# Attention, mixer and MLP block on one core: output-weight slices in other heads, and a rebuilt opening

## The chip, the cores and the metric

The kernel runs on one core of a Trainium2 chip. The metric is device time in microseconds (us), the median over several runs. The engines are named as the profile names them: PE is TensorE's matrix products, PEld its weight loads, DVE is VectorE, ACT is ScalarE, POOL is GpSimd and SP is SyncE, which here only issues DMAs. A name with a q (SPq) is the engine's own instruction queue. PSUM is the memory that TensorE writes its results to; everything else on the core lies in SBUF.

## The reference

The input x has 2048 rows of 640. A vector c gives six modulation rows of 640 through `silu(c) @ w_mod`. An attention with 32 heads over a given cache of 2048 keys follows, then a mixer and an MLP.

```python
mod = (_silu(c) @ w_mod).reshape(c.shape[0], 6, 1, -1)
sa, ca, ga, sb, cb, gb = (mod[:, 0].copy(), mod[:, 1].copy(), ...)
h = _layernorm(x, axis=-1) * (1 + ca) + sa
x = x + ga * _A_ref(h, A_k_cache, A_v_cache, A_wq, A_wo)
h = _layernorm(x, axis=-1) * (1 + cb) + sb
x = x + gb * _B_ref(h, B_w1, B_w2, B_w3, B_w4)
...
def _A_ref(x, k_cache, v_cache, wq, wo):      # H, Dh = 32, 128
    q = (lambda x, *d: x.transpose(*d))((x @ wq).reshape(B, Sq, H, Dh), 0, 2, 1, 3)
    scores = jnp.einsum('bhqd,bhkd->bhqk', q, k_cache) * Dh ** (-0.5)
    p = _softmax(scores, axis=-1)
    o = jnp.einsum('bhqk,bhkd->bhqd', p, v_cache)
    return (lambda x, *d: x.transpose(*d))(o, 0, 2, 1, 3).reshape(B, Sq, H * Dh) @ wo
```

`_B_ref` is a layernorm, a product with w1, GELU, a shift of column groups by one or two rows, a product with w2, and a second layernorm with the MLP (w3, GELU, w4).

## The kernel before

**Order of work.** A small class, `Prog`, takes operations for the five engines in program order, with the keys that each reads and writes, and turns every dependence between two engines into a semaphore wait. Within an engine the operations run in the order in which they were given. All loads and all transposes by DMA are issued from one queue, SP's; the writes of finished attention rows go out from POOL's queue.

**Attention.** The loop over `s` (L691) has 512 steps: 32 heads of 16 tiles of 128 query rows. In a step TensorE computes 128 x 2048 scores in two halves into PSUM (`qk`, L344); DVE scales each half into SBUF and takes its row minimum of the negated scores (L725); POOL joins the two minima (L735); ACT takes the exponential into the buffer `Pb`, eight steps deep (L738). The probabilities are transposed, mostly two steps at a time, by a DMA from SP's queue (`transpose`, L263); 8 to 10 steps later TensorE multiplies them with V (`pv`, L357), ACT copies the result out of PSUM (L679) and POOL normalises and stores it (L592, L599, L606). Beside the steps of one head stand the loads of the next ones (K at L748, the slice of wq at L750, V at L752) and the Q projection of the next head, in twenty pieces (`q_piece`, L277, emptied by ACT in `q_evac`, L284).

**The output weights.** `wo` (4096 x 640) is loaded in 16 slices of two heads each, 320 KB a slice (`load_wo`, L376). `WO_AT` (L688) says in which head, at step 11, which slice is issued: two in head 0, then one in every odd head from 1 to 27. Their space serves the opening first: the later part of w_mod, statistics and small vectors lie in it. Every operation that uses it so reads the keys `WRK`, and a slice's load waits for those.

**The opening** (L394 to L520) computes what the first scores need: layernorm statistics of x (`bn` and `aggr` on DVE, per tile two BATCH_NORM_STATS2 over 320 columns and one aggregate), the reciprocal root (`rs`: for the first four tiles Sqrt on ACT and a reciprocal on DVE, for the others two operations on POOL), the normalised rows (`xhat`), their transposes on TensorE (`tr`), and the modulated, transposed rows hT (`ev`, on ACT or DVE, from PSUM). `ev` needs the two modulation columns `mcol`: fifty small products on TensorE (`cols`, L423) from the first part of w_mod and silu(c), then two ACT operations (L509, L510). Then `q_head0` makes the first 512 columns of head 0's Q. Loads are issued in the order x(0), c, x(1), w_mod's first part, x(2), wq(0), K(0), x(3), wq(1), V(0), w_mod's rest; x(cc) is 512 rows, 640 KB. The vector c is loaded as 128 x 5 single elements.

**Head 0** carries the rest of that work as side work, placed by hand in the table `PLAN` (L327). Keys of `q1`, `own`, `mod` and `tr` are half steps `u` (two a step) in TensorE's queue: `q1` the Q pieces of head 1, `own` the remaining Q pieces of head 0, `mod` the modulation rows (`mod_rows`, L575), `tr` the transposes. `es` and `evv` place the evacuations on ACT and DVE; `bn` the statistics; `xv` and `xg` the normalisation of a tile on DVE or on POOL, by step. `within` (L522) runs a half step's TensorE part, `ahead` (L537) the ACT part before the step's exponential, `beside` (L547) the DVE and POOL part behind it.

**Tail.** From L764 on: the output projection, the mixer and the MLP, with TensorE busy almost throughout.

Of the kernel before, what the change touches and what calls it, by code (L numbers as in the profile page):

```python
# [151 lines left out]
def bass_adaLN_cond__mha_block_cached__mixer_s_mlp__prompt_kernel(  # L152
# [6 lines left out]
    KT = D // 128  # L159
# [14 lines left out]
    with ExitStack() as es:  # L174
# [11 lines left out]
        if True:  # L186
            with ExitStack() as es1:
# [44 lines left out]
                c_sb = wof[:, CO + 6 * KT:CO + 7 * KT]  # L232
                s_col = wof[:, CO + 7 * KT:CO + 8 * KT]
                assert CO + 8 * KT <= H * D and SK + 8 * D <= WO_ and WO_ + KT * 2 * D <= 10 * SK
# [85 lines left out]
                for cc in range(NQC):  # L320
# [84 lines left out]

                G.op("gpsimd", lambda g: g.memset(ident[:], 0.0), w=["id0"])
# [5 lines left out]
                eps_f, mh_f = pad[:, 0:4], pad[:, 4:8]  # L412
                G.op("gpsimd", lambda g: g.memset(eps_f, 0.0), w=["warm"])
                G.op("gpsimd", lambda g: g.memset(mh_f, -0.5), w=["mh"])
                G.op("scalar", lambda a: a.activation(s_col, c_sb, ACT.Silu), r=["c"], w=["scol"])
                G.op("scalar", lambda a: a.activation(c_f, c_sb, ACT.Silu), r=["c"], w=["cf"])
# [19 lines left out]
                def aggr(cc):  # L436
                    for t in range(4 * cc, 4 * cc + 4):
                        G.op("vector", lambda v, t=t: v.bn_aggr(mv[:, t, :], st[:, t, :]),
                             r=[("st", t, 0), ("st", t, 1)] + WRK, w=[("mv", t)])

                def rs(cc):
                    c4 = slice(4 * cc, 4 * cc + 4)
                    if cc == 0:
                        G.op("scalar", lambda a: a.activation(sd[:, c4], mv[:, c4, 1], ACT.Sqrt, bias=float(EPS)),
                             r=[("mv", t) for t in range(4 * cc, 4 * cc + 4)], w=[("sd", cc)])
                        G.op("vector", lambda v: v.reciprocal(rstd[:, c4], sd[:, c4]), r=[("sd", cc)], w=[("rstd", cc)])
                    else:
                        G.op("gpsimd", lambda g: g.tensor_scalar(out=sd[:, c4], in0=mv[:, c4, 1], scalar1=float(EPS), scalar2=1.0,
                                                                 op0=ALU.add, op1=ALU.mult),
# [51 lines left out]
                for k in range(KT - 1):  # L501
                    tr(0, (k,), Sps[:, k * 512:(k + 1) * 512].bitcast(BF16), ("Sb", k))
# [571 lines left out]
```

## Time and profile before

| | us |
|---|---|
| median of 3 runs | 1537.18 (1533.27 to 1546.02) |
| the profiled execution | 1542.95 |
| its span, first to last instruction | 1541.2 |
| first attention reduction on DVE (L725) | 20.55 from the span's start |
| first one of head 1 | 66.01 |
| start of the last of all | 1211.6 |

The profile is of one execution. The page lists the busy time of each engine; the other views are questions to the same trace: its instructions in order of time, busy time by stretch, who waited for whom (total us, times, longest), and the DMA issues with the time from issue to landing. An instruction is written as engine, line, operation, output<-input; in the view by time the first number is its start and the second its length in us, and instructions of one kind that follow each other are merged (x4). A wait for several semaphores is put down to the one that came last. The granted TensorE clock was 1.000 throughout.

The loads of the opening, from the DMA issues of short stretches: x(0) issued at 0.74, landed 4.2 later; c at 1.25, 5.3; x(1) at 1.80, 6.9; w_mod's first part at 2.36, 10.4; x(2) at 2.91, 11.5; wq(0) at 4.47, 10.5; K(0) at 6.12, 10.8; x(3) at 14.91, 4.9.

### The profile page before, as it was taken

How to read it: one execution, taken by the hardware profiler on the slowest of the kernel's cores; microseconds unless marked ns; L12 is line 12 of the kernel's file. 1: busy time of each engine (PE TensorE's matmuls, PEld its weight loads, DVE VectorE, ACT ScalarE, POOL GpSimd, SP SyncE). 2: the span in 40 equal slices, each digit the busy share in tenths (PEclk: the TensorE clock that was granted, in tenths of full speed). 3: DMA queues.
4: the chain of work that ended last, by engine and by line, in shares of the span. 5: the costliest groups of instructions: out<-in, count | busy, mean ns of one | idle time of the engine just before them, and what ended most of it. 6: DMA issues, size and time to landing. Idle time of an engine off the chain costs nothing.

```text
span 1541.2 us, 36159 instructions
## 1 busy us (share of the span) xinstructions
PE 1491.6 (97%) x14087; PEld 951.2 (62%) x14087; DVE 1372.1 (89%) x2425; ACT 1240.7 (81%) x1141; POOL 644.7 (42%) x1409
## 2 busy tenths in 40 slices
PE   5999999999999999999999999999999999999999
PEld 2566666666666666666666666666666665544444
DVE  8999999999999999999999999999999556676324
ACT  6999999999999999999999999999999500044230
POOL 4344444444444444444444444444444433332100
PEclk9999999999999999999999999999999999999999
DMA  9999999999999999999999999999999997635100
GB/s 280 226 244 227 250 257 249 247 251 249 253 244 255 242 251 248 253 248 258 243 242 256 251 252 253 260 253 254 263 243 225 226 219 169 131 85 105 34 17 35
DMA packets 1187333, 337.08 MB, mean 219 GB/s; under 512 B 1167984, under 2 KB 1181232, under 8 KB 1187248
## 3 DMA queue, kind: packets, MB, share of 16 engines
q1 hardware_dynamic: 1181104, 319.31, 99.6%
q0 software_dynamic: 6144, 16.79, 3.9%
q8 instruction: 35, 0.57, 0.2%
q14 instruction: 50, 0.41, 0.1%
HBM read 43.48 MB, written 19.40 MB: 41 GB/s over the span
## 4 chain that ended last, share of the span: by engine, by line
ACT 28%; DVE 25%; PE 24%; DMA 11%; issue 11%; POOL 0%; SPq 0%; ACTq 0%; DVEq 0%; POOLq 0%
DVE negS L725 24%; ACT ring L738 22%; DMA ring<-ring 9%; PE Sps L795 9%; PE Sps L996 4%; ACT ring L306 2%; ACT Of L679 2%; PE Oaug L980 2%; PE QPp L980 2%; PE PTp L364 2%; ACT kv L287 1%; PE Sps L962 1%; PE Sps L351 1%; DMA hTx<-o_scratch 1%; PE QPp L867 1%
## 5 line engine op out<-in xcount | busy, mean ns | idle before, releaser
L725 DVE TENSOR_SCALAR_CACHE_REDUCE negS<-Sps 128x1024 f32<-128x1024 f32 x1024 | 1174.7, 1219 | 10.8 <-PE Sps L351 10.0
L738 ACT ACTIVATE ring<-negS,small 128x2048 bf16<-128x2048 f32 x512 | 1039.2, 2050 | 23.5 <-DMA ring<-ring 11.4
L364 PEld LDWEIGHTS PTp<-kv,ring 128*128 128x128 bf16 x8192 | 555.9, 98 | 259.6 <-issue 14.0
L364 PE MATMUL PTp<-kv,ring 128*128 128x129 bf16 x8192 | 644.1, 220 | 15.0 <-DMA ring<-ring 13.8
L351 PE MATMUL Sps<-kv 128*128 128x512 bf16 x2048 | 616.8, 383 | 15.4 <-DVE negS L725 5.6
L735 POOL TENSOR_SCALAR small<-small 128x1 f32<-128x1 f32 x512 | 147.2, 287 | 570.5 <-DVE negS L725 570.3
L351 PEld LDWEIGHTS Sps<-kv 128*128 128x128 bf16 x2048 | 132.3, 97 | 149.9 <-DVE negS L725 125.0
L599 POOL TENSOR_SCALAR On<-Of,small 128x128 bf16<-128x128 f32 x512 | 192.0, 376 | 13.0
L592 POOL TENSOR_TENSOR small<-Of,small 128x4 f32<-128x4 f32 x128 | 133.2, 1041 | 22.5 <-ACT Of L679 22.5
L280 PE MATMUL Oaug<-hTx,kv 128*128 128x512 bf16 x320 | 120.5, 381 | 1.4 <-ACT hTx L481 1.4
L606 POOL DMA_DIRECT2D o_scratch<-On x128 | 103.2, 806 | 40.8 <-POOL On L599 37.2
L679 ACT COPY Of<-PTp 128x259 f32<-128x259 f32 x256 | 104.6, 409 | 18.9 <-PE PTp L364 18.9
L280 PE MATMUL QPp<-hTx,kv 128*128 128x512 bf16 x320 | 119.2, 378 | 0.6 <-DMA kv<-in_A_wq_dram 0.6
L875 ACT ACT_TABLE_LOAD x1 | 1.3, 1283 | 104.2 <-POOL hTx L923 104.2
L725 DVE DVE_READ_ACCUMULATOR negS<-Sps 128x1 f32 x1024 | 84.8, 83 | 0.0
L776 POOL TENSOR_SCALAR negS<-negS 128x1 f32<-128x1 f32 x48 | 24.1, 503 | 118.2 <-DVE negS L785 118.0
L795 PE MATMUL Sps<-wo,hTx 128*128 128x512 bf16 (+1 forms) x512 | 70.5, 299 | 0.2 <-DMA hTx<-o_scratch 0.2
L1013 DVE TENSOR_TENSOR ring<-Sps,ring 128x640 f32<-128x640 f32 x15 | 12.4, 824 | 65.5 <-PE Sps L996 65.5
L795 PE MATMUL Sps<-wo,negS 128*128 128x128 bf16 (+1 forms) x512 | 70.4, 299 | 0.0
L807 DVE TENSOR_TENSOR ring<-Sps,mod_bc 128x640 f32<-128x640 f32 x16 | 13.1, 821 | 51.3 <-PE Sps L795 51.3
L795 PEld LDWEIGHTS Sps<-wo,negS 128*128 128x128 bf16 x512 | 39.6, 98 | 30.4
L795 PEld LDWEIGHTS Sps<-wo,hTx 128*128 128x128 bf16 x512 | 39.4, 98 | 30.3 <-DMA hTx<-o_scratch 0.4
(99 smaller groups left out, 994.7 us busy)
## 6 DMA issues: line engine op xcount, KB each, us to landing
kv<-in_A_v_cache_dram SPq DMA_DIRECT2D x32, 512.0 KB, 4.9
o_scratch<-On POOLq DMA_DIRECT2D x128, 128.0 KB, 5.2
ring<-in_A_x_dram SPq DMA_DIRECT2D x8, 640.0 KB, 5.0
kv<-in_A_wq_dram SPq DMA_DIRECT2D x32, 160.0 KB, 3.2
wo<-in_A_wo_dram SPq DMA_DIRECT2D x16, 320.0 KB, 5.3
ring<-ring SPq DMA_TRANSPOSE x254, 6.5
wo<-in_w_mod_dram SPq DMA_DIRECT2D x1, 3200.0 KB, 15.0
out_dram<-wo SPq DMA_DIRECT2D x16, 160.0 KB, 1.8
```

What stands on the lines that cost most here:

```text
L280: G.op("tensor", lambda t: t.matmul(JB[jb], wq[:, hb, q, :], hT[:, q, cc * 512:(cc + 1) * 512], start=(q == 0), stop=(q == KT - 1)), r=[(" ...
L351: ins = t.matmul(Sps[:, col:col + 512], QT[:, hb, j * 128:(j + 1) * 128], KTs[:, hb, col:col + 512], start=True, stop=True)
L364: ins = t.matmul(ob[:, 0:129], PTs[:, b, kt, :], Vaug[:, hb, kt, 0:129], start=(kt == 0), stop=(kt == NKT - 1))
L592: G.op("gpsimd", lambda g: g.tensor_tensor(out=rl[:, 4 * b:4 * b + 4], in0=Of[:].rearrange("p a z d -> p (a z) d")[:, 4 * b:4 * b + 4, 128 ...
L599: G.op("gpsimd", lambda g: g.tensor_scalar(out=On[:, b, z, :], in0=Of[:, 2 * b + z // 2, z % 2, 0:128], scalar1=rl[:, 4 * b + z:4 * b + z ...
L606: G.dma("gpsimd", lambda e: e.dma_start(o_scr[jj // 2:jj // 2 + 2, :, hh].rearrange("a p z d -> p a (z d)"), On[:, b].rearrange("p (a z) d ...
L679: G.op("scalar", lambda a: a.copy(Of[:, p % 4].rearrange("p z d -> p (z d)")[:, 0:259], PO[:, (p % 2) * 512:(p % 2) * 512 + 259]), r=[("O" ...
L725: G.op("vector", lambda v, half=half, s=s, r8=r8: v.tensor_scalar(out=negS[:, s % 3, half * 1024:(half + 1) * 1024], in0=Sps[:, half * 102 ...
L735: G.op("gpsimd", lambda g, r8=r8: g.tensor_scalar(out=nm[:, r8:r8 + 1], in0=nm0[:, r8:r8 + 1], scalar1=nm1[:, r8:r8 + 1], scalar2=None, op ...
L738: G.op("scalar", lambda a, s=s, r8=r8: a.activation(Pb[:, s % RPB, :], negS[:, s % 3, :], ACT.Exp, bias=nm[:, r8:r8 + 1], scale=-1.0), r=[ ...
L795: ins = t.matmul(YB[b][:, c0:c0 + cw], OTj[pr % 2][:, 2 * hh + z, :], wo[:, hh, c0:c0 + cw], start=(hh == 0), stop=(hh == H - 1))
L980: ins = t.matmul(JB[jb][0:fsz[f_], :], w3[:, k, f_ * 128:f_ * 128 + fsz[f_]], nT[:, k, cc * 512:(cc + 1) * 512], start=(k == 0), stop=(k = ...
```

## The change

Four parts:

1. **Slices.** `WO_AT` issues the 16 slices in heads 5, 6, 8, 9, 11, 12 and so on to 26, 27, one a head.
2. **Loads.** x(0), x(1) and x(2) are issued first, then c, w_mod's first part, wq(0), x(3), K(0) and the rest as before. c is loaded as five rows of 128, turned into columns by one TensorE transpose (`c_cols`), and the two Silu read PSUM. 
3. **Statistics.** For tiles 3, 6, 7 and 11 ACT sums the row (Identity with an accumulator), POOL makes the negative mean, ACT sums the squares of x plus that (Square with an accumulator), and POOL makes mean and variance. The reciprocal root of the first four tiles moves to POOL's two operations, so ACT's Sqrt and DVE's reciprocal go. Twenty-four products of the identity with itself (`warm`) are put in TensorE's queue, ten ahead of c's transpose and fourteen behind it. The order of the opening is rewritten; the s columns that `mod_rows` needs (`spread_s`) move behind the third group's statistics on POOL, mcol's two copies behind ACT's last sum of squares; the first group's evacuations are three on DVE and two on ACT instead of two and three; tile 12's statistics come into the opening, and the second group's transposes and evacuations leave it.
4. **Table.** `PLAN` is new: the second group's transposes at half steps 0 and 1 with their five evacuations on ACT in step 0; DVE normalises tiles 8, 11, 14, 15 and 13, POOL 10, 9 and 12 (before: DVE 8, 11, 15; POOL 10, 9, 12, 13, 14); statistics of 13 to 15 in steps 2 and 3; Q pieces and modulation rows moved by a few half steps.

```diff
+                def junk():
+                    nj[0] += 1
+                    assert nj[0] <= NJ
+                    return wof[:, JU + (nj[0] - 1) * D:JU + nj[0] * D]
...
-                    q1={0: (3, 4, 6, 6, 7), 1: (14, 16, 16, 16, 17), 2: (15, 17, 17, 17, 17), 3: (25, 26, 29, 30, 30)},
-                    own={1: (2, 2, 3, 5, 5), 2: (10, 11, 12, 12, 12), 3: (22, 22, 22, 23, 23)},
-                    mod=[(9, 3, 2), (11, 2, 1), (14, 3, 0), (16, 3, 1), (18, 2, 1)],
-                    tr={0: (1, (4,), 1), 6: (2, (0, 1), 2), 7: (2, (2, 3), 1), 8: (2, (4,), 0), 18: (3, (0, 1), 0), 19: (3, (4,), 2), 21: (3, (2, 3), 1)},
-                    es={0: [(1, (4,))], 3: [(2, (2,)), (2, (0,)), (2, (1,))], 4: [(2, (3,))], 10: [(3, (4,))]},
+                    q1={0: (3, 4, 4, 5, 7), 1: (14, 14, 15, 16, 17), 2: (15, 15, 16, 16, 16), 3: (26, 28, 30, 30, 31)},
+                    own={1: (2, 3, 4, 5, 5), 2: (10, 11, 11, 12, 12), 3: (22, 22, 22, 22, 23)},
+                    mod=[(9, 3, 2), (12, 3, 1), (14, 3, 0), (16, 2, 1), (18, 2, 1)],
+                    tr=[(0, 1, (0, 1), 2), (0, 1, (4,), 2), (1, 1, (2, 3), 0), (6, 2, (0, 1), 2), (7, 2, (2, 3), 1), (8, 2, (4,), 0), (19, 3, (0, 1), 0), (19, 3, (4,), 2), (21, 3, (2, 3), 1)],
+                    es={0: [(1, (0, 1, 2, 3)), (1, (4,))], 3: [(2, (0,)), (2, (1,)), (2, (2,))], 4: [(2, (3,))], 10: [(3, (4,))]},
                     evv={4: [(2, (4,))], 9: [(3, (0,)), (3, (1,))], 10: [(3, (2, 3))]},
-                    bn={1: (12,), 2: (13, 14, 15)},
-                    xv={0: (8, 11), 8: (15,)},
-                    xg={0: (10,), 1: (9,), 3: (12,), 5: (13,), 7: (14,)},
+                    bn={2: (13, 14), 3: (15,)},
+                    xv={0: (8,), 1: (11,), 7: (14, 15), 8: (13,)},
+                    xg={0: (10,), 1: (9,), 4: (12,)},
...
-                    with nc.allow_non_contiguous_dma(reason="tiny c vector"):
-                        return e.dma_start(c_sb, c[0].rearrange("(kt p) -> p kt", p=128))
-                load_x(0)
+                    return e.dma_start(c_row, c[0].rearrange("(k p) -> k p", p=128))
+                for cc in range(3):
+                    load_x(cc)
                 G.dma("sync", load_c, "c", w=["c"])
-                load_x(1)
                 load_mod(0, wmod, 0, 2 * D)
-                load_x(2)
                 load_wq(0)
+                load_x(3)
                 load_k(0)
-                load_x(3)
...
+                def c_cols():
+                    G.op("tensor", lambda t: t.transpose(ctr, c_row, ident[0:KT, 0:KT]), r=["c", "ident"] + WRK, w=[("J", 0)])
+                    G.op("scalar", lambda a: a.activation(s_col, ctr, ACT.Silu), r=[("J", 0)] + WRK, w=["scol"])
+                    G.op("scalar", lambda a: a.activation(c_f, ctr, ACT.Silu), r=[("J", 0)] + WRK, w=["cf"])
+
+                def warm(n, key):
+                    def f(t):
+                        for _ in range(n):
+                            ins = t.matmul(JB[0][:, 0:128], ident[:], ident[:], start=True, stop=True)
+                        return ins
+                    G.op("tensor", f, r=["ident", key], w=[("J", 0)])
+
+                def sum_x(t):
+                    dst = junk()
+                    G.op("scalar", lambda a: a.activation(dst, xs(t), ACT.Identity, accum_out=sums[0][:, t:t + 1]),
+                         r=[("x", t // 4)] + WRK, w=[("sum", t)])
+
+                def sum_sq(t):
+                    dst = junk()
+                    G.op("scalar", lambda a: a.activation(dst, xs(t), ACT.Square, bias=sums[1][:, t:t + 1], accum_out=sums[2][:, t:t + 1]),
+                         r=[("x", t // 4), ("nmean", t)] + WRK, w=[("ssq", t)])
+
+                def nmean(t0, t1):
+                    G.op("gpsimd", lambda g: g.tensor_scalar(out=sums[1][:, t0:t1], in0=sums[0][:, t0:t1], scalar1=-1.0 / D, scalar2=1.0,
+                                                             op0=ALU.mult, op1=ALU.mult),
+                         r=[("sum", t) for t in range(t0, t1)] + WRK, w=[("nmean", t) for t in range(t0, t1)])
...
-                bn(0, 4)
-                aggr(0)
+                bn(0, 3)
+                aggr(0, 3)
+                sum_x(3)
+                nmean(3, 4)
+                sum_sq(3)
+                mean_var(3, 4)
                 rs(0)
+                warm(10, ('mv', 1))
+                sum_x(6)
+                sum_x(7)
+                sum_x(11)
+                c_cols()
+                warm(14, ('mv', 1))
+                nmean(6, 8)
+                nmean(11, 12)
+                sum_sq(6)
+                sum_sq(7)
+                mean_var(6, 8)
+                bn(4, 6)
+                aggr(4, 6)
+                rs(1)
                 xhat("vector", 0, 4)
+                tr0()
+                bn(8, 11)
                 G.op("scalar", lambda a: a.activation(eps_f, eps_f, ACT.Exp), r=["warm"], w=["warm"])
...
+                sum_sq(11)
+                mean_var(11, 12)
+                mcol_of()
+                aggr(8, 11)
+                rs(2)
                 spread_s()
...
+                xhat("vector", 4, 6)
+                ev("vector", 0, (0, 2, 4))
+                ev("scalar", 0, (1, 3))
                 q_head0(0)
...
+                xhat("vector", 6, 8)
+                bn(12, 13)
...
-                WO_AT = {0: (0, 1), **{h: (h // 2 + 2,) for h in range(1, 2 * NWP - 4, 2)}}
+                WO_AT = {5 + i // 2 * 3 + i % 2: (i,) for i in range(NWP)}
```

`mean_var` is two POOL operations that scale the two sums by 1/640 into the tile's mean and variance; `mcol_of` holds the column products and the two ACT operations as before; `tr0` the first group's transposes as before.

More of the change, by code (lines that the diff above doesn't have):

```diff
@@ L411, in bass_adaLN_cond__mha_block_cached__mixer_s_mlp__prompt_kernel @@
                 G.op("gpsimd", lambda g: g.memset(Vaug[:, :, :, 128:130], 1.0), w=["ones"])
[L412 to L416, printed above, removed]
+                ctr = JBb[0][:, 0:KT]
@@ L442, in rs @@
                     c4 = slice(4 * cc, 4 * cc + 4)
[L443 to L449, printed above, removed]
[L450 to L452 removed]
+                    G.op("gpsimd", lambda g: g.tensor_scalar(out=sd[:, c4], in0=mv[:, c4, 1], scalar1=float(EPS), scalar2=1.0,
+                                                             op0=ALU.add, op1=ALU.mult),
+                         r=[("mv", t) for t in range(4 * cc, 4 * cc + 4)], w=[("sd", cc)])
+                    G.op("gpsimd", lambda g: g.tensor_tensor(out=rstd[:, c4], in0=sd[:, c4], in1=mh_f, op=ALU.pow),
+                         r=[("sd", cc), "mh"], w=[("rstd", cc)])
                 def xhat(eng, t0, t1):
@@ L494, in q_head0, with mcol_of, tr0 @@
                         q_evac(0, cc)
-                bn(0, 4)
-                aggr(0)
-                rs(0)
+                def mcol_of():
+                    G.op("tensor", cols, r=["scol", ("wm", 0)] + WMK + WRK, w=[("J", 1)])
+                    G.op("scalar", lambda a: a.copy(mcol[:, 0:KT], JB[1][:, 0:KT]), r=[("J", 1)], w=["mcol0"])
+                    G.op("scalar", lambda a: a.add(mcol[:, KT:2 * KT], JB[1][:, KT:2 * KT], 1.0), r=[("J", 1), "mcol0"], w=["mcol"])
+                def tr0():
+                    for k in range(KT - 1):
+                        tr(0, (k,), Sps[:, k * 512:(k + 1) * 512].bitcast(BF16), ("Sb", k))
+                    tr(0, (KT - 1,), OB[0], ("O", 0))
@@ L554, in beside @@
                         if t == NQT - 1:
-                            aggr(3)
+                            aggr(12, 16)
                             rs(3)
```

54 lines of the change are left out of this document (25 added, 29 removed).

## The prediction

> **What bounds the kernel now.** I began with the page's busy shares. They are an average over an opening, 512 attention steps and a tail on TensorE, so I read stretches next.
>
> ```profile
> PE 1491.6 (97%) x14087; PEld 951.2 (62%) x14087; DVE 1372.1 (89%) x2425; ACT 1240.7 (81%) x1141; POOL 644.7 (42%) x1409
> ```
>
> ```profile
> 658.00:807.00 149.00, 144.54 (x1483) 97.02 (x1480) 146.83 (x257) 145.58 (x129) 70.03 (x160) 1.00 1.20 247
> ...
> 954.00:1101.00 147.00, 145.86 (x1498) 96.93 (x1496) 147.00 (x259) 147.00 (x129) 70.05 (x161) 1.00 1.20 255
> ```
>
> Columns: length, then busy time of PE, PEld, DVE, ACT, POOL. From 954 to 1101 DVE has no idle time: attention runs at DVE's pace, two reductions a step. The timeline shows that pace, and where it starts:
>
> ```profile
> 20.55 1.17 DVE L725 TENSOR_SCALAR_CACHE_REDUCE negS<-Sps 128x1024 f32<-128x1024 f32 x1
> ```
>
> ```profile
> 998.98 1.22 DVE L725 TENSOR_SCALAR_CACHE_REDUCE negS<-Sps 128x1024 f32<-128x1024 f32 x1
> ...
> 1001.27 1.22 DVE L725 TENSOR_SCALAR_CACHE_REDUCE negS<-Sps 128x1024 f32<-128x1024 f32 x1
> ```
>
> A step is 1001.27 - 998.98 = 2.29 us. The same view has head 1's first reduction at 66.01. Head 0 takes 66.01 - 20.55 = 45.46, of which 16 x 2.289 = 36.62 is its reductions and 8.84 side work and idle time. From 66.01 to the start of the last reduction (1211.6) there are 495.5 steps: 1134.2 at that pace, 1145.6 in fact, so 11.4 us of stalls. The waits name them:
>
> ```profile
> PE PTp L364 <- DMA ring<-ring: 13.8, 19, 1.2
> ```
>
> TensorE's second product waits for the transposes of the probabilities, and DVE then waits for the next scores (10.0 us in 20 waits). The tail from 1212.8 on is bound by TensorE and is not touched. So the change can act in three places: the 20.55 us before the first reduction, head 0's 8.84, and the 11.4 of stalls.
>
> **The opening.** DVE before the first reduction: 8 statistics 3.25 + 3.24 + 3.24 (three groups of four tiles), aggregates 3 x 0.41, reciprocal 0.18, xhat 1.52 + 1.51, two evacuations 0.99: 15.2 us after x lands at 4.94. After: statistics of nine tiles (0 to 2, 4, 5, 8 to 10, 12) at 0.81, 7.3; eight aggregates at 0.10, 0.8; eight xhat, 3.0; three evacuations, 1.5: 12.6. If DVE never waited, the first reduction would start at 17.6, a gain of 2.9.
>
> DVE now depends on ACT, whose rows before are
>
> ```profile
> 6.94 1.28 ACT L444 ACT_TABLE_LOAD   x1
> 8.57 0.20 ACT L444 ACTIVATE small<-small 128x4 f32<-128x4 f32 x1 [0.34 <-DVE small L438]
> 8.79 1.28 ACT L500 ACT_TABLE_LOAD   x1
> 10.09 0.20 ACT L500 ACTIVATE pad<-pad 128x4 f32<-128x4 f32 x1
> ```
>
> The next row starts at 14.33, so ACT was idle for 4 us there. After, in its order: sum and square of tile 3, sums of 6, 7, 11, two Silu behind a table load, squares of 6 and 7, the Exp load, square of 11, then mcol's two copies. A pass over 640 elements with an accumulator is in no row. From below: 512 elements cost 0.59 (the Q evacuation) and 2048 cost 2.00, so 640 cost 0.71. From above: the 512-element evacuation with two pointer operands at 0.77, plus 0.12 for the length, plus 0.08 as DVE pays to read its accumulator: 0.97. I take 0.80, nearer to the lower end, since the 2048-element row reads SBUF as these do. The chain: 4.96 + 5 x 0.80 + 0.3 (POOL's 0.20 for the negative mean, and two hand-offs) = 9.3; load and Silu 1.28 + 0.4 = 10.9; two squares 12.5; Exp 1.28 + 0.2 = 14.0; square of 11 14.8; mcol at 15.2, where it was at 14.70.
>
> TensorE's 50 column products (1.49) wait for the first part of w_mod. Its queue:
>
> ```profile
> ring<-in_w_mod_dram SPq DMA_DIRECT2D x1, 1600.0 KB, 10.4
> ...
> wo<-in_c_dram SPq DMA_DIRECT2D x1, 1.2 KB, 5.3
> ```
>
> ```profile
> 4.00:5.00 1.00, 0.00 (x0) 0.00 (x0) 0.04 (x1) 0.00 (x0) 0.00 (x0) 1.00 0.65 143
> 5.00:6.00 1.00, 0.00 (x0) 0.00 (x0) 1.00 (x3) 0.00 (x0) 0.00 (x0) 1.00 0.57 121
> ```
>
> The last column is GB/s. While c's 1.2 KB is loaded element by element the queue moves some 130, against 420 from 8 to 9: 1.4 us lost. As five rows that loss goes (at worst it stays); the third x load, now ahead of w_mod, adds 655 KB / 410 = 1.6. So w_mod lands at 12.76 + 0.2 = 12.9, at worst 14.4, and the columns end at 14.4 to 15.9. K of head 0, which landed at 16.9, has the fourth x load moved past it on SP (+1.6) and c's loss taken out: 17.0, at worst 18.5.
>
> From mcol at 15.2: evacuations 1.5 (DVE three, ACT two), last Q product and its evacuation 0.4 + 0.6, hand-offs 0.1, scores 0.6: 18.4. DVE, after its evacuations, does xhat of 6 and 7 and tile 12's statistics (0.76 + 0.81) and ends at 18.3. So the first reduction would start at 18.4; with 0.97 per pass 1.4 later, with w_mod at worst 0.7 later. I take 19.0, as hand-offs between five engines are likelier to add than to save: **-1.5 us**, bounds -2.8 (0.71 a pass) and 0 (both at their worst).
>
> Waits it adds: on ACT, Silu waits for c's transpose, which on TensorE stands behind ten warming products waiting for tile 1's aggregate (7.7); behind Silu stand the squares, Exp and mcol. On POOL the negative mean of 11 waits for x's third load, and behind it are the variances of 6 and 7 and the power (1.05, row of the 128x4 power) that releases xhat 4 and 5: 12.5 + 0.4 + 0.2 + 1.05 = 14.2, before DVE's evacuations can start at 15.2, so hidden by one us. The power for tiles 0 to 3 replaces a table load, Sqrt and reciprocal (1.7 together): even. The s columns move on POOL behind three such groups and end near 19; their first reader ran at 34.17. Warming products and memsets fill idle time: nothing, and at most 24 x 0.117 (the first 16 transposes took 1.87) = 2.8 if the tiles' transposes were ready at once.
>
> **Head 0.** DVE gets two more xhat (0.4 to 0.6 each) and one tile's statistics fewer (-0.81): 0 to +0.4. Five evacuations of the second x group (0.70 each) now stand on ACT ahead of the first Exp, which starts near 23.0 instead of 23.44: ACT gains less than DVE. It has 3.7 us idle from 24 to 60, so it can follow, but TensorE's shared PSUM banks are emptied by ACT, and 20 transposes (1.5) join its steps. The new table's idle time is in no row: -1.0 to +1.5. I take **+0.3**.
>
> **The slices.** Two leave head 0, one each heads 1 and 3; the rest stand in two heads of three from 5. On SP's queue, two cycles from V to V:
>
> ```profile
> 919.88 0.59 SPq L253 DMA_DIRECT2D kv<-in_A_v_cache_dram  x1
> 920.50 1.40 SPq L377 DMA_DIRECT2D wo<-in_A_wo_dram  x1
> ...
> 956.69 0.59 SPq L253 DMA_DIRECT2D kv<-in_A_v_cache_dram  x1
> ...
> 992.48 0.60 SPq L253 DMA_DIRECT2D kv<-in_A_v_cache_dram  x1
> ```
>
> 36.81 with a slice, 35.79 without: a slice costs the queue about 1.0, and the queue is full against a head of 36.62. By head 4 the queue has carried four slices fewer; from 5 to 27 it carries two in three heads instead of one in two. Stalls may fall by up to 4 x 1.0, or rise by (2/3 - 1/2) x 1.0 x 23 = 3.8. What is saved early is mostly paid late: **-0.5**.
>
> **Sum.** -1.5 + 0.3 - 0.5 = -1.7. The profiled execution took 1542.95 (span 1541.2), which gives 1541.2; it lies 5.8 above the median of three runs, 1537.18. I apply the difference to the median: **1535.5**.
>
> **Rivals.** (1) ACT's chain becomes the bound, and it is slower. Square stands after Silu and again after Exp; rows show that Identity and Copy run after Exp with no new load, none shows it for Square. Three more loads at 1.28 put mcol at 19.0, 3.2 later the first reduction at 22.2 and, with head 0 and the slices as above, the end 1.5 later than before: 1539. It decides from the second such load on (21.0 against 20.55). Against it: the simple functions have needed no load so far. Chance 0.17. (2) The denser slices keep the transposes late through heads 5 to 27: +3.8, with the opening's gain 1540. For it: heads around 480 to 810 stall with slices; against it: heads without slices stall too. 0.12. (3) The early slices were what began the lag, and nearly all stalls go. The fastest run before, 1533.27, is 9.7 below the profiled one and so has few; less 1.7 that is 1531.5. 0.13. (4) The opening is rebuilt but w_mod and K land at their worst and it gains nothing: 1537, 0.07. [...] Chance 0.03. [...]
>
> **Numbers.** Forecast 0.48, rivals 0.17, 0.12, 0.13, 0.07 and 0.03. About 1%, 15 us, is what a measurement of this kernel can tell from no change (three runs spread over 13). No case reaches it: within 0.95; 0.02 faster and 0.03 slower for what I have not named. The range takes (3) with the best opening, 1528, and (2) with the spread of the runs, 1545.
>
> **What would show it.** First reduction near 19.0 (after 20.5: the opening failed); mcol near 15.2; one table load for Silu and one for Exp, none for Square; nine tiles of statistics on DVE before it; head 0 within 45.5 to 46.5; no slice before head 5 on SP, and 7 to 12 us of stalls after head 0. I am wrong if one wait in head 0 passes 3 us, or if stalls leave 3 to 16.

## The result, and the profile after

The kernel after takes 1531.66 us (median of 22 runs, 1530.67 to 1542.33), the kernel before 1540.53 on the same chips (22 runs, 1531.96 to 1550.10). The ratio is 0.9956, with a 95% interval of 0.9938 to 0.9973: a gain that the measurement resolves, but one of less than 1%.

The single times say more than the medians. Of before's 22, seven lie within 1531.96 to 1533.68 and fifteen from 1537.18 up. Of after's 22, twenty lie within 1530.67 to 1532.59. The bulk of the gain is thus that long executions have become rare; between the best groups of the two kernels there is about 1 us.

The profiled execution after took 1531.64 (span 1529.8); before's span was 1541.2. Cut at the same places as in the prediction, the 11.4 us between the two spans come from:

| | before | after | difference |
|---|---|---|---|
| first reduction on DVE | 20.55 | 20.20 | -0.35 |
| head 0, first reduction to head 1's first | 45.46 | 45.78 | +0.32 |
| head 1's first reduction to the end of the last | 1146.8 | 1135.9 | -10.9 |
| the tail behind it | 328.4 | 327.9 | -0.5 |

496 steps at 2.289 us are 1135.3, so 0.6 us of stalls are left where before had 11.5. In before, the 30 heads from 1 to 30 exceed 16 steps of 2.289 (36.62 us) by 9.4 in all, the longest taking 38.18; in after each of them takes 36.62. The busy times of the page, and the two stretches of attention that the prediction read (length, then busy time of PE, PEld, DVE, ACT, POOL, then granted clock, DMA share, GB/s):

```profile
PE 1476.2 (96%) x13867; PEld 948.8 (62%) x14112; DVE 1368.0 (89%) x2415; ACT 1249.1 (82%) x1155; POOL 640.8 (42%) x1418
```

```profile
658.00:807.00 149.00, 145.65 (x1486) 98.13 (x1511) 149.00 (x261) 149.00 (x131) 71.59 (x164) 1.00 1.16 255
954.00:1101.00 147.00, 143.66 (x1468) 96.81 (x1492) 147.00 (x259) 147.00 (x130) 70.03 (x161) 1.00 1.16 255
```

In the first stretch DVE was idle for 2.17 us before, and is not idle now. The waits of after no longer have a line for TensorE's second product waiting on the transposes (13.8 us in 19 waits before), and DVE's wait for scores is down from 10.0 us in 20 waits to this (total, times, longest):

```profile
DVE negS L787 <- PE Sps L362: 2.8, 3, 1.3
```

L787 is the reduction that was L725, L362 the score products. One of the three stands late in head 0 (0.65 at 56.83), two in the opening, as its DVE rows show (start, length, and in brackets the idle time ahead of it and what ended that):

```profile
18.06 0.87 DVE L477 BATCH_NORM_STATS2 wo<-ring 128x6 f32<-128x320 bf16 x2
20.20 1.22 DVE L787 TENSOR_SCALAR_CACHE_REDUCE negS<-Sps 128x1024 f32<-128x1024 f32 x1 [1.28 <-PE Sps L362]
...
22.34 1.22 DVE L787 TENSOR_SCALAR_CACHE_REDUCE negS<-Sps 128x1024 f32<-128x1024 f32 x1 [0.90 <-PE Sps L362]
```

DVE had finished its part of the opening at 18.9 (forecast 18.3), and then waited for TensorE. The opening lost its expected gain there; the chain on ACT was not what held it:

```profile
4.88 0.74 ACT L440 ACTIVATE wo<-ring 128x640 bf16<-128x640 bf16 x1 [2.87 <-DMA ring<-in_A_x_dram]
5.52 0.19 ACT L440 ACTIVATION_READ_ACCUMULATOR wo<-ring 128x1 f32 x1
6.02 0.83 ACT L445 ACTIVATE wo<-ring,wo 128x640 bf16<-128x640 bf16 x1 [0.31 <-POOL wo L449]
...
9.11 1.28 ACT L428 ACT_TABLE_LOAD   x1
10.40 0.18 ACT L428 ACTIVATE wo<-Oaug 128x5 bf16<-128x5 bf16 x1
...
12.28 1.28 ACT L569 ACT_TABLE_LOAD   x1
...
13.68 0.81 ACT L445 ACTIVATE wo<-ring,wo 128x640 bf16<-128x640 bf16 x1
...
15.71 0.17 ACT L538 ACTIVATE wo<-QPp 128x5 f32<-128x5 f32 x1
```

A sum over 640 costs 0.74 and 0.19 for reading the accumulator, overlapping by 0.10: 0.83 by itself. Passes that follow each other overlap again, and the next begins 0.72 later for a sum (6.84, 7.56, 8.28) and 0.81 later for a square (10.53, 11.34); 0.80 was taken for each. Square (L445) runs behind Silu's load (10.53, 11.34) and behind Exp's (13.68) without one of its own. The last square ends at 14.49, its accumulator is read by 14.59; 14.8 was forecast. But mcol (L538) comes at 15.88 instead of 15.2, and from mcol to the first reduction it is 4.3 us; the forecast was 3.2, and 3.8 with the allowance for hand-offs. Both are TensorE's rows, in the same view:

```profile
10.70 1.67 PE L434 MATMUL Oaug<-ident 128*128 128x128 bf16 x14 [1.70 <-ACT wo L429]
12.17 1.85 PE L509 MATMUL Sps<-ident,ring 128*128 128x128 bf16 x16
...
14.07 1.40 PE L470 MATMUL QPp<-wo,ring 128*128 128x1 bf16 x50
16.82 1.63 PE L291 MATMUL Oaug<-hTx,kv 128*128 128x512 bf16 x4 [1.35 <-ACT hTx L520]
19.13 1.03 PE L362 MATMUL Sps<-kv 128*128 128x512 bf16 x2 [0.68 <-ACT kv L298]
```

The fourteen warming products (L434) write the bank that the Silu read, wait for that until 10.70, and run to 12.37; the first group's transposes (L509) stand behind them, although their rows were ready at 10.75. They start 1.4 us late, and with them the column products (L470) and mcol. Then the scores: two products take 1.03 and one takes 0.61 to 0.63, where before's took 0.38. The stretches of 1 us show why, in the column of the granted clock (third from the end):

```profile
16.00:17.00 1.00, 0.18 (x1) 0.22 (x3) 1.00 (x3) 1.00 (x2) 0.90 (x3) 1.00 1.00 227
17.00:18.00 1.00, 1.00 (x4) 0.20 (x3) 1.00 (x3) 0.36 (x1) 1.00 (x4) 0.61 1.18 260
18.00:19.00 1.00, 0.45 (x2) 0.00 (x0) 0.93 (x3) 0.51 (x1) 0.36 (x1) 0.50 1.45 239
...
23.00:24.00 1.00, 1.00 (x5) 0.40 (x3) 0.93 (x3) 0.81 (x2) 0.34 (x1) 0.50 1.03 430
24.00:25.00 1.00, 0.74 (x4) 0.10 (x1) 0.95 (x1) 1.00 (x2) 1.00 (x2) 0.97 1.01 420
```

The trace's clock records stand at 13.8 (full), 17.2 (half) and 24.1 (full again): 3.4 us and two times 3.4 us apart. In the 3.4 us up to 17.2 TensorE was busy for about 60%, with one gap of 1.35 us before L291. So in this execution the full clock was there and was lost just ahead of the scores.

The same opening is in seven more traces, of runs shown below. In four of them (old places; one slice a head; four early; eight early) the first clock record stands at 13.5 to 15.0, the full clock is lost 3.4 us later as here, and the first reduction comes at 20.30 to 20.76. In the other three (two early slices; the old spacing from head 5; the kernel after once more) there is no record before 22.9, the first score products take 0.61 to 0.63, and the first reduction comes at 20.97 to 21.23. Over these eight traces the opening gains nothing on before's 20.55, and in three of them the warming products did not bring the full clock in time at all.

The loads did as forecast. The two stretches in which before moved 143 and 121 GB/s, while c was loaded element by element, now read

```profile
4.00:5.00 1.00, 0.00 (x0) 0.00 (x0) 0.12 (x1) 0.12 (x1) 0.00 (x0) 1.00 1.06 392
5.00:6.00 1.00, 0.00 (x0) 0.00 (x0) 1.00 (x3) 0.70 (x2) 0.21 (x2) 1.00 1.06 396
```

and w_mod's first part lands at 12.22 (forecast 12.9), K of head 0 at 16.45 (17.0).

### The profile page after: what moved, and what is told of

The parts are those of the page before. It is cut to its first block, busy times and chain, and to the rows that moved or that the text cites. A ratio compares the mean times of both kernels' runs of the same rounds, so it can differ in the third digit from the quotient of the medians.

```text
span 1529.8 us, 35980 instructions
## 1 busy us (share of the span) xinstructions
PE 1476.2 (96%) x13867; PEld 948.8 (62%) x14112; DVE 1368.0 (89%) x2415; ACT 1249.1 (82%) x1155; POOL 640.8 (42%) x1418
## 4 chain that ended last, share of the span: by engine, by line
DVE 63%; PE 23%; issue 11%; ACT 3%; DMA 0%; POOL 0%
DVE negS L787 62%; PE Sps L857 9%; PE Sps L1058 4%; PE Oaug L1042 2%; PE QPp L1042 2%; ACT ring L800 1%; PE Sps L1024 1%; PE PTp L375 1%; PE Sps L362 1%; PE QPp L929 1%; PE Oaug L929 1%; ACT hTx L937 0%; ACT kv L298 0%; DMA ring<-in_A_x_dram 0%; PE Oaug L291 0%
## 5 line engine op out<-in xcount | busy, mean ns | idle before, releaser
L787 DVE TENSOR_SCALAR_CACHE_REDUCE negS<-Sps 128x1024 f32<-128x1024 f32 x1024 | 1173.2, 1221 | 3.5 <-PE Sps L362 2.8
L800 ACT ACTIVATE ring<-negS,small 128x2048 bf16<-128x2048 f32 x512 | 1025.3, 2020 | 6.6 <-POOL small L797 6.5
L362 PE MATMUL Sps<-kv 128*128 128x512 bf16 x1946 | 597.8, 385 | 31.3 <-DVE negS L787 7.9
L362 PEld LDWEIGHTS Sps<-kv 128*128 128x128 bf16 x2048 | 118.7, 97 | 162.1 <-DVE negS L787 150.5
L741 ACT COPY Of<-PTp 128x259 f32<-128x259 f32 x256 | 97.4, 381 | 18.9 <-PE PTp L375 18.9
L291 PE MATMUL QPp<-hTx,kv 128*128 128x512 bf16 x274 | 102.1, 378 | 0.0
L291 PE MATMUL Oaug<-hTx,kv 128*128 128x512 bf16 x259 | 97.4, 380 | 2.1 <-ACT hTx L520 2.1
L787 DVE DVE_READ_ACCUMULATOR negS<-Sps 128x1 f32 x1024 | 85.7, 84 | 0.0
L857 PE MATMUL Sps<-wo,negS 128*128 128x512 bf16 (+1 forms) x505 | 69.3, 298 | 0.4
L857 PE MATMUL Sps<-wo,hTx 128*128 128x128 bf16 (+1 forms) x503 | 69.2, 298 | 0.5
```

The lines of the kernel that those rows point to most:

```text
L291: G.op("tensor", lambda t: t.matmul(JB[jb], wq[:, hb, q, :], hT[:, q, cc * 512:(cc + 1) * 512], start=(q == 0), stop=(q == KT - 1)), r=[(" ...
L362: ins = t.matmul(Sps[:, col:col + 512], QT[:, hb, j * 128:(j + 1) * 128], KTs[:, hb, col:col + 512], start=True, stop=True)
L741: G.op("scalar", lambda a: a.copy(Of[:, p % 4].rearrange("p z d -> p (z d)")[:, 0:259], PO[:, (p % 2) * 512:(p % 2) * 512 + 259]), r=[("O" ...
L787: G.op("vector", lambda v, half=half, s=s, r8=r8: v.tensor_scalar(out=negS[:, s % 3, half * 1024:(half + 1) * 1024], in0=Sps[:, half * 102 ...
L800: G.op("scalar", lambda a, s=s, r8=r8: a.activation(Pb[:, s % RPB, :], negS[:, s % 3, :], ACT.Exp, bias=nm[:, r8:r8 + 1], scale=-1.0), r=[ ...
L857: ins = t.matmul(YB[b][:, c0:c0 + cw], OTj[pr % 2][:, 2 * hh + z, :], wo[:, hh, c0:c0 + cw], start=(hh == 0), stop=(hh == H - 1))
```

## Where the stalls went: the lead of the transposes

The place to look is not the length of a head but how early a transpose lands. From the trace's DMA issues, each with its time to landing, I worked out the lead of each transpose: the start of the reduction of the step in which TensorE first uses that tile, less the landing. This is the smallest lead in each head, in us, by the head that the probabilities belong to; those of its last steps are used some 10 steps later, in the next head:

```
head                    0     1     2     3     4     5   later heads
before                6.9   4.0   0.9  -0.1   1.0   1.2   -0.7 to 0.6 through 20, then up to 4.2 in 29
after                 9.1   5.8   4.0   3.3   4.8   4.3    3.4 to 5.5 to 29
```

In both kernels the lead falls from head to head at first: by 2.9, 3.1 and 1.0 before, by 3.3, 1.8 and 0.7 after. Before's falls to nothing and stays there for nearly twenty heads, in which a slice or another delay can become a stall; after's stops falling at 3.3. On SP's queue after's first transpose is issued earlier (29.19 against 31.50), but by 62.7 the two queues are level. From there they differ, at head 0's two slices in before and at the same place in after (time, duration, instructions merged):

```profile
62.68 0.59 SPq L248 DMA_DIRECT2D kv<-in_A_wq_dram  x1
63.31 2.34 SPq L377 DMA_DIRECT2D wo<-in_A_wo_dram  x2
65.69 16.50 SPq L265 DMA_TRANSPOSE ring<-ring  x4
```

```profile
62.67 0.58 SPq L259 DMA_DIRECT2D kv<-in_A_wq_dram  x1
63.93 16.41 SPq L276 DMA_TRANSPOSE ring<-ring  x4
```

The issue of the slices alone puts the next four transposes 1.8 us later, and four slices have gone by before head 4. That is the theory which the first runs test. Its rivals: the stalls went with the rebuilt opening; or they depend on how dense the slices are, not on where the first ones stand.

## The experiments

In each, the kernel before was run on the same chip in between, and the ratio is to that. Before's share of long executions differs between these groups of runs, which were on different chips: fifteen of 22 above, but 14 of 35, 9 of 26 and 12 of 29 above 1534.5 in the groups below, where its medians are 1533.40 to 1533.46. So a ratio near 0.998 there and 0.9956 above can belong to the same kernel, and for stalls I read the spread and the leads beside the ratio.

### Slices alone, opening alone

The kernel before with only the new places of the slices:

```diff
-    WO_AT = {0: (0, 1), **{h: (h // 2 + 2,) for h in range(1, 2 * NWP - 4, 2)}}
+    WO_AT = {5 + i // 2 * 3 + i % 2: (i,) for i in range(NWP)}
```

> The kernel before with one line changed: the 16 slices of the output weights in heads 5 to 27. Theory A (the four early slices start the lateness of the transposes that later stalls DVE): every head from 1 on takes 36.6 us, the first reduction stays at 20.5 us, head 1 starts at 66, the time is 1530 to 1533. Theory B (the earlier loads of the rebuilt opening start the transposes earlier, 29.2 instead of 31.5 us, and that is what keeps them ahead): heads of 37 to 38 us remain between 3 and 21 and the time stays near 1540, as before.

Measured: 1532.95 (12 runs, 11 of them at most 1534.2, one at 1538.73), ratio 0.9987 (0.9972 to 1.0003); before's 35 runs reach 1543.2. First reduction at 20.51, head 1 36.90, heads from 2 on 36.62 each, smallest lead 9.2, 7.1, 3.3, 3.1, 4.5 in heads 0 to 4 and at least 3.1 to head 30.

The kernel after with the old places (the same two lines exchanged):

> The changed kernel with the old places of the slices (two in head 0, then the odd heads to 27). Theory A: stalls return, several heads between 3 and 21 take 37 to 38 us, 1538 to 1542. Theory B: every head 36.6 us, 1531 to 1533.

Measured: 1538.28 (12 runs, 9 of them above 1534.5, up to 1545.9), ratio 1.0026 (1.0006 to 1.0046): slower than before. Its profile happened to be of its best execution (1531.75), which has no long head; but its lead is 5.8, 4.4, 2.8, 2.2, 1.7, 1.1, 0.9, 0.4 in heads 0 to 7, stays between 0.3 and 1.2 to head 19, and is back at 3.1 only in head 24. What follows: the stalls come and go with the places of the slices, and the new opening does not remove them. That the opening with the old places does worse than before wasn't explained.

### Early places or dense places

Five runs move slices within the kernel after. Two in head 0, the others as in after:

```diff
-    WO_AT = {5 + i // 2 * 3 + i % 2: (i,) for i in range(NWP)}
+    WO_AT = {0: (0, 1), **{5 + i // 2 * 3 + i % 2: (i,) for i in range(2, NWP)}}
```

> The changed kernel with slices 0 and 1 back in head 0 and the other 14 where the change put them (8 to 27). Theory A in its strong form (what is issued in head 0 decides): stalls return, 1536 or more. Theory A in its weak form (about one us of queue per slice, eaten from a lead of some 3 to 4 us): two slices take 2 us of the lead, the smallest lead goes from 3.3 to near 1.3 us and no head is longer than 36.7 us, 1531 to 1533. Theory B: 1531 to 1533.

Measured: 1532.69 (12 runs, 11 of them at most 1533.54, one at 1542.98), 0.9986 (0.9967 to 1.0005); lead 6.0, 4.4, 2.6, 2.7, 3.9, 5.1, where 1.3 was expected as the smallest. Two early slices cost the first heads 1 to 3 us of lead and leave no stall on the transposes: head 1 is 0.3 longer (36.95), as in the two runs above, but there TensorE waits 0.3 to 0.4 us for wq.

One slice in each of sixteen heads on end:

```diff
+    WO_AT = {12 + i: (i,) for i in range(NWP)}
```

> The changed kernel with one slice in every head from 12 to 27, a denser order than either kernel has. If the density of slices is what makes the transposes late (the second rival of the prediction), heads 14 to 27 take 37 us or more and the time is 1536 or more. If the early heads decide, no head is longer than 36.7 us and the time is 1531 to 1533.

Measured: 1532.05 (12 runs, 1531.32 to 1532.69), 0.9981 (0.9968 to 0.9994). Every head takes 36.62, and in heads 12 to 27, with a slice in each, the smallest lead is 3.1 to 4.4. The density cost nothing here, where the lead was there first.

The old spacing of every second head, but from head 5, with the last four in heads 20 to 26:

```diff
+    WO_AT = {**{5 + 2 * i: (i,) for i in range(12)}, **{20 + 2 * i: (12 + i,) for i in range(4)}}
```

> The changed kernel with no slice before head 5, twelve in the odd heads from 5 to 27 as the kernel before has them, and the four that were early in heads 20, 22, 24 and 26. It takes the early slices alone from the old places. If the early ones decide: the lead stays at 3 us or more to head 19, every head takes 36.6 us, 1531 to 1533. If the odd heads are what keeps the transposes late (a rival that the run with all the old places left open): the lead falls to about 1 us by head 10, stalls in many executions, 1535 or more.

Measured: 1532.04 (12 runs, 1530.91 to 1532.82), 0.9982 (0.9971 to 0.9993); all heads from 1 on 36.62, lead at least 3.0 to head 29. So the old spacing is harmless too, without the four slices ahead of head 5.

The other way round, those four in their old heads and the others as in after:

```diff
+    WO_AT = {0: (0, 1), 1: (2,), 3: (3,), **{5 + i // 2 * 3 + i % 2: (i,) for i in range(4, NWP)}}
```

> The changed kernel with the old places for the four early slices alone (two in head 0, one each in heads 1 and 3), the other twelve where the change put them (11 to 27). If the early ones eat the lead and it comes back where no slice follows: the lead falls to 1 to 2 us at heads 3 and 4 and is above 3 us again by head 8, before the next slice, with few stalls: 1531.5 to 1534. If the four early ones alone explain the whole loss: 1537 or more, as with all the old places.

Measured: 1534.87 (12 runs, 1532.77 to 1538.8, 7 of them above 1534.5), 1.0006 (0.9992 to 1.0021); the unchanged kernel after, on the same chip (below), takes 1531.75. In the profile heads 3, 4 and 5 take 37.94, 36.68 and 37.75, and the lead is 5.3, 1.6, -1.0, 0.3, -0.8, 1.2, 2.0, 2.6, 3.1 in heads 0 to 8. Four early slices use up the lead and cause stalls; with no slice in heads 4 to 10 the lead is back at 3 by head 8. (A lead below nothing in heads 2 and 4 is a stall in heads 3 and 5.) The time lies between the two that were expected: the four early slices cost 3 us here, less than all the old places did on another chip (1538.28). Since the old spacing alone is harmless, the rest must come from both together, early slices that use up the lead and a slice in every second head behind them; how the second keeps it low wasn't shown.

Eight slices early, two in each of heads 0 to 3, and eight from head 20 on:

```diff
+    WO_AT = {0: (0, 1), 1: (2, 3), 2: (4, 5), 3: (6, 7), **{12 + i: (i,) for i in range(8, NWP)}}
```

> The changed kernel with two slices in each of heads 0 to 3 and the other eight in heads 20 to 27. Theory A in its weak form (a slice eats about one us of the transposes' lead, and stalls begin when the lead is gone): eight slices eat all of the 3 to 5 us, the lead is near zero from head 2 or 3, and the stalls show in most executions: 1536 to 1545. If the early slices were not what began the stalls, 1531 to 1533.

Measured: 1541.03 (4 runs, 1538.01 to 1542.23), 1.0039 (1.0023 to 1.0054). The stretches are about one head each, heads 2 to 5:

```profile
103.00:140.00 37.00, 35.45 (x364) 23.88 (x361) 36.32 (x63) 34.87 (x32) 17.43 (x40) 1.00 1.18 236
140.00:182.00 42.00, 37.78 (x379) 26.61 (x380) 36.90 (x65) 38.06 (x34) 17.52 (x40) 0.96 1.20 245
182.00:223.00 41.00, 37.82 (x378) 25.87 (x375) 36.99 (x65) 36.92 (x33) 17.52 (x40) 0.96 1.18 244
223.00:260.00 37.00, 36.72 (x377) 24.30 (x375) 37.00 (x67) 37.00 (x33) 17.64 (x41) 1.00 1.15 251
```

and its waits, TensorE's and DVE's:

```profile
PE PTp L375 <- DMA ring<-ring: 8.2, 4, 3.6
```

```profile
DVE negS L787 <- PE Sps L362: 11.9, 11, 3.7
```

DVE's 37 us of work take 42 and 41 us in heads 3 and 4: the second product waits for the transposes, DVE for the scores behind it. The lead is 5.4, -0.5, -3.1, -2.4 in heads 0 to 3, 2.7 again in head 4, and above 3.5 from there to head 29; from head 5 on every head takes 36.62. The stalls themselves give the queue time, and no slice follows until head 20. Just behind the two longest the clock is lower as well: 0.96 on average in each stretch, from records of 0.50 for 3.4 us at 158.4 (TensorE had waited 3.63, up to 157.52) and at 199.3 (DVE's idle time ahead of 200.03 is 2.88).

The unchanged kernel after, once more, on the chip of the runs with the old spacing and with four early slices:

> The changed kernel itself, on the chip of these runs: 1531 to 1533, the measure for the other runs. If it is near 1535 here, the executions with stalls belong to the chip and not to the kernel.

Measured: 1531.75 (12 runs, 1530.97 to 1532.82), 0.9982 (0.9971 to 0.9994), before's median being 1533.40 here.

### The opening: warming and filling

Both `warm` calls taken out:

```diff
-                warm(10, ('mv', 1))
...
-                warm(14, ('mv', 1))
```

> The changed kernel without its 24 warming products. The fourteen behind c's transpose waited there for the two Silu (10.65) and stood ahead of the first group's transposes, which began at 12.17 though their rows were ready at 10.75. Theory C (they cost more than they give): the transposes begin at 10.8, mcol is ready near 15.0 instead of 15.88, the first reduction starts between 19.0 and 19.6 instead of 20.2, and the time is 1530 to 1531. Theory D (without them TensorE stays at half its clock longer): the first scores take 0.6 us a product, the first reduction stays at 20 or later, 1531.5 to 1533.

Measured: 1531.68 (11 runs, ten within 1531.4 to 1531.88, one at 1540.98), 0.9983 (0.9964 to 1.0002). Transposes from 10.89 instead of 12.17, mcol's copies done at 14.95 instead of 15.88, but the first reduction only 0.5 earlier, at 19.72. The score products are still slow:

```profile
10.89 1.89 PE L509 MATMUL Sps<-ident,ring 128*128 128x128 bf16 x16 [2.11 <-DVE ring L495]
...
18.64 1.03 PE L362 MATMUL Sps<-kv 128*128 128x512 bf16 x2 [0.68 <-ACT kv L298]
```

The stretches give the clock as 1.00 here, from 13 to 24, though one product takes 0.61 to 0.63: the first clock record stands at 23.0, and ahead of the first record the column says 1.00 for want of one. The duration of a product is the surer sign. Head 1 begins 0.5 earlier and gives 0.45 back (37.07 long, a Q piece waits 0.5 us for wq). So the fourteen products do hold up the transposes, but in this execution, without any warming, TensorE stays at half clock up to 23.0. The lead is lower here, though no slice has moved: 1.7, 1.4, 2.2, 2.3, 1.2 in heads 2 to 6. Places of slices are not the only thing that sets it, and even so no head from 2 on is lengthened.

Both calls kept, ten more products behind mcol and six behind head 0's Q, in banks that are free there (`warm` gets the bank as an argument):

```diff
                 mcol_of()
+                warm(10, ('mv', 1))
...
                 q_head0(0)
+                warm(6, ('mv', 1), 1)
```

> The changed kernel with ten more warming products behind the column products and six behind head 0's first Q pieces, where TensorE was idle for 1.35 and 0.7 us before its granted clock fell to 0.50 at 17.2. Theory E (the idle time let the clock fall, and the half clock cost the 2.3 us for which DVE waited for its first scores): the clock stays at 1.00 past 17, the first score products take 0.38 us instead of 0.61, DVE waits under 1 us instead of 2.3 between 18 and 24, head 1 starts near 64.5 and the time is 1530 to 1530.5. Rival F (ACT is behind in head 0 anyway, and what DVE wins is lost before head 1): head 1 starts at 65.7 to 66 as before, 1531.5.

Measured: 1530.90 (11 runs, 1529.88 to 1531.3), 0.9973 (0.9961 to 0.9984), a little above the expected 1530.5. The clock reaches 1.00 at 14.8 and keeps it:

```profile
17.00:18.00 1.00, 1.00 (x4) 0.33 (x5) 1.00 (x3) 0.72 (x2) 1.00 (x4) 1.00 1.06 236
...
20.00:21.00 1.00, 1.00 (x16) 0.76 (x14) 1.00 (x3) 0.85 (x2) 0.00 (x0) 1.00 0.84 102
```

A score product takes 0.38 to 0.39 and DVE's idle time ahead of the first reduction is 0.40 instead of 1.28. First reduction 19.70, head 0 44.80 (45.78 in after), head 1 at 64.50 instead of 65.99.

The same without the fourteen products ahead of the transposes:

```diff
-                warm(14, ('mv', 1))
```

> As the run with the sixteen more, but without the fourteen behind c's transpose. If theories C and E both hold: mcol near 15.0, first reduction between 18.6 and 19.3, head 1 at 63.8 to 64.5, 1529 to 1530, the best of these. If only F holds: head 1 near 65.8, 1531.5.

Measured: 1530.19 (10 runs, 1529.55 to 1530.77), 0.9976 (0.9967 to 0.9985), a little above the expected 1530; span 1527.8. TensorE's rows:

```profile
10.98 1.89 PE L509 MATMUL Sps<-ident,ring 128*128 128x128 bf16 x16 [1.80 <-DVE ring L495]
...
14.47 1.23 PE L434 MATMUL Oaug<-ident 128*128 128x128 bf16 x10
15.75 2.15 PE L291 MATMUL Oaug<-hTx,kv 128*128 128x512 bf16 x5
17.74 0.50 PE L434 MATMUL QPp<-ident 128*128 128x128 bf16 x6
18.58 0.61 PE L362 MATMUL Sps<-kv 128*128 128x512 bf16 x2 [0.34 <-ACT kv L298]
```

The transposes start when their rows are there, the filling products stand only in gaps, the clock is full from 17.6, and two score products take 0.61 together where after's took 1.03. First reduction at 19.22, head 1 at 64.02: 1.97 less than after, and 2.0 is what the span gains. On the same chip the run without warming took at least 1531.40, and the ten executions here take at most 1530.77; the kernel after itself was not run there, and its best executions elsewhere reach 1530.67. The two runs with filling products are not told apart by their ratios, but by their single times: six of the first one's eleven lie above 1530.77. Both profiles are of executions from the faster part of their run (1530.17 and 1529.59), so it is not shown that the clock held in all of them. By its median this is the best kernel of the study.

## Why the time was right and the reasons half wrong

The time (1531.66, forecast 1535.5 within 1528 to 1545) and "within 1%" held. The likeliest case did not: what happened is the third rival (early slices began the lag, 1531.5), which had a chance of 0.13. That the time came near is in part luck. The forecast was a gain of 1.7, and the medians differ by 8.9; it was taken from the median of three runs of before, 1537.18, and over 22 runs that median is 1540.53, from which the same sum would give 1538.8. The third rival's 1531.5 is also luck in part, since it counts 1.5 for the opening, which did not come.

- **ACT's chain: right.** 14.59 against 14.8; one load each for Silu and Exp, none for Square. That removes the rival of ACT as the bound. For the last chance in the list of rivals, 0.03, no run shows a case: a table load held ACT for its 1.28, and the ACTIVATE behind it started about 0.01 after its end (loads at 9.11 and 12.28, ACTIVATEs at 10.40 and 13.57). The passes took 0.72 to 0.74 for a sum and 0.81 to 0.83 for a square.
- **Loads: right.** Both landed 0.6 earlier than forecast; the rival in which they hold up everything falls.
- **"Warming products and memsets fill idle time: nothing": failed.** That step had named the case, an upper bound of 2.8 if the transposes were ready at once, and chose zero. They were ready at 10.75 and waited 1.4 us; with the gaps behind filled, the fourteen cost 0.5 us at the first reduction (19.70 with them, 19.22 without). The products were also given a value of nothing, while the clock decides how long the scores take (1.03 us for two at half clock, 0.61 at full clock).
- **3.2 us from mcol to the first reduction: failed, 4.3.** The sum took the scores at full clock, since the clock column of before reads 1.00 from the start. But the first clock record of before stands at 18.8, just ahead of its scores, and ahead of a first record the column proves nothing. The 0.6 that was added for hand-offs covers half of the 1.1 that were missing. The runs with filling products show the price: keeping the clock and the queue free brings the first reduction to 19.22, near the 19.0 of the forecast. So -1.5 is about the size of the opening done that way (19.22 against 20.55 is -1.3). As it was built it measured -0.35 in the profiled execution, and -0.35 to +0.7 over the eight traces; in five of them the first reduction comes after 20.5, the prediction's own sign that the opening failed.
- **Head 0: right**, +0.32 against +0.3. The runs with filling show that 1.0 of its 45.78 us can still be had; part of it is the half clock up to 24.1 and DVE's second wait of 0.90 (with the half clock over by 20.4 to 21.8, in the runs with the old places, with four and with eight early slices, head 0 takes 44.86 to 45.35). How the rest divides wasn't taken apart.
- **"What is saved early is mostly paid late: -0.5": failed, -10.9 in the profiled execution.** The price of a slice on SP's queue (about 1.0) was of the right order: two in head 0 cost 1 to 3 us of lead in the first heads. The fault was to add such prices up as if the queue's balance were all that counted. A lead of 3 us or more absorbed a slice in every head for sixteen heads, at no cost (36.62 a head, smallest lead 3.1 to 4.4); with a lead near zero lateness became stalls (42 and 41 us for heads 3 and 4 with eight early slices). So saving four early and paying later is no exchange of equals. The rival of the denser slices falls with the run of one slice a head.

The prediction's own signs spoke at once: no slice before head 5 was right, but "7 to 12 us of stalls after head 0" met 0.6, and "first reduction near 19.0" met 20.20. It had called itself wrong if stalls left 3 to 16.

Open: why the lead falls behind head 0 in both kernels; why it is lower in the two runs without the fourteen products ahead of the transposes (1.4 and 2.1 in head 3); why a lost lead is back within some five heads when no slice follows, but takes twenty with the old places, although a lead of 3 to 4 us holds under a denser load; why before's long executions are more frequent in some groups of runs; and what makes the few long ones that are left with the new places (two of after's 22), of which no profile was taken.

## What to carry to other kernels

For a queue that runs nearly full, work out the lead of its transfers over their first use, step by step, and put extra loads where the lead is steady, not where it is still falling: here a slice in each of sixteen heads cost nothing at a lead of 3.1 us or more, and four slices ahead of head 5 cost 3 us. The mean load of the queue did not tell. Put a product that is meant to keep TensorE's clock up into a gap ahead of real work, never in front of work that is ready (the fourteen cost 0.5 us at the first reduction), and fill the gap behind it too (first reduction at 19.22 that way, 20.20 as built). Compare the duration of equal products before you believe a clock column: one of 0.61 to 0.63 us stood under a column of 1.00, where the full clock gave 0.38.

## What the runs showed of the hardware

The changes of the granted clock that the records show lie 3.4 us or twice that apart (13.8, 17.2 and 24.1 in after; half clock for 3.4 us, twice, in the run with eight early slices), and they fall at other places in each execution (the first record at 13.5 to 15.0 or at 22.9 to 23.7 with the same opening). In after, a stretch with TensorE busy for about 60%, its longest gap 1.35 us, was followed by half clock; in the run with filling products, one of about 84% from 14.8 to 18.2 was followed by full clock. These traces give no threshold, though. The stretch after the loss, about 80% busy at half clock, was followed by half clock in after and with one slice a head, and by full clock with the old places, with four and with eight early slices. And later stretches no busier were followed by full clock: 46% with a gap of 1.83 us in before from 29.0, 54% with one of 1.51 in the run with four early slices from 150.1. What else counts, such as the fifty products of one column in the lost stretch, wasn't tested.

In these traces a score product of 512 columns alone takes 0.61 to 0.63 at half clock and 0.38 at full clock. That is less than double, but a second one behind it adds 0.42 (1.03 for two) or 0.23 (0.61 for two): the pace is about halved, and by that difference, an estimate, 0.15 to 0.2 us of each single duration is the same at both clocks. Reading an accumulator cost ACT 0.18 to 0.20 us, DVE 0.08 to 0.09.
